# Local attention and MLP in one kernel: logits issued by pairs against logits issued after all products, subtraction in PSUM, and a new order of the work

## The chip, the cores and the metric

The kernel runs on one core of a Trainium2 chip. The metric is the device time of one execution in microseconds, lower is better. Engines are named as in the profile: PE does the matmuls (PEld its weight loads), DVE is the vector engine, ACT the scalar engine, POOL and SP mainly issue DMAs here.

## What is computed

x has 2048 rows of 640 bf16 numbers. With xn = layernorm(x), the output is x + A(xn) + B(xn).

```python
# A: 32 heads of 20 numbers; each row looks at 8 rows, 0, 2, ... 14 rows back
q, k, v = split(xn @ wqkv)                       # [32, 2048, 20] each
logits = einsum("bhsd,bhswd->bhsw", q, k[rows s - 2*w]) * 20 ** -0.5
logits = where(s - 2*w >= 0, logits, -1e9)
attn = softmax(logits over w)                    # w = 0..7
A = einsum("bhsw,bhswd->bhsd", attn, v[rows s - 2*w]) @ wo
# B: an MLP with 1536 hidden numbers
B = gelu_tanh(xn @ w1 + b1) @ w2 + b2
```

## The kernel before, in words

The 2048 rows are cut into four chunks of 512 (n = 0 to 3), each of four blocks of 128 rows (bl). Everything is held transposed: 128 partitions carry a slice of the 640 features (in five slices, t), the free axis carries the chunk's rows. The work is cut into 569 pieces, each a closure that issues a few instructions. A hand-held list, `ORDER`, gives the order in which all pieces are issued; every engine executes its own pieces in just that order, waiting by semaphore for what the pieces read and for the buffers they write. (`make_plan` also holds a cost and a rank for each piece, but when `ORDER` is given only the pieces' functions are used. POOL is not in the list of engines whose order is fixed by hand.) A piece's name is its kind, the chunk, and an index:

- `st`, `rs`, `rc`, `xn`, `tc`: row statistics (DVE, L403), square root (ACT, L424), reciprocal (DVE, L428), normalised rows (ACT, L440), and the transposing DMA into `xnT` (SP, L471). In chunk 0 matmuls transpose instead (`tp`), and its projections are cut smaller (`ga` to `ge`, `hj`, with their copies `gc`, `hc`).
- `pj n which to`: five matmuls of 128x512 for one slice of q, k or v (which = 0, 1, 2; PE, L503), and `pc`: its copy out of PSUM to bf16 (ACT, L562). `pad`: the 14 rows carried over from the chunk before.
- `qk n wp i`: q times k shifted by 2*(2*wp+i) rows, 2560 numbers per partition (DVE, L577), into a `prod` tile; one tile holds the pair i = 0, 1, so a chunk has four. The pool has four such tiles.
- `lg n wp`: the sums over each head: matmuls with a 128x32 matrix of zeros and ones (PE, L599), 256 columns each, in four column strips, 20 of them for each wp, into the PSUM tile `L` (one buffer, 8 offsets x 128 columns). In the kernel before, `lg03` does all 80 of chunk 0; in the other chunks `lg n1` does the 40 of wp 0 and 1, and `lg n3` those of wp 2 and 3.
- softmax: `mk` the mask of chunk 0 (L594), `m` the maximum (L612), `mx` the subtraction (L619), all DVE; `ex` the exponential (ACT, L629); `ss`, `ri`, `at` sum, reciprocal and product (DVE, L635 to L647).
- `xd`, `xs`: the attention weights are spread over partitions by four DMAs into `ax` (one buffer): two issued by SP (`xd`), two by ACT (`xs`, L657).
- `av n wp i`: v shifted, times `ax` (DVE, L673), into `prod` tiles; `ad` adds tiles pairwise (DVE, L682; three for a chunk), `ot` makes the result `oT` (DVE, L688).
- `f1 n ft`: five matmuls of 128x512 for one of twelve hidden slices (PE, L695), `ge`: gelu (ACT, L706), into `hT`.
- `o n bl pc`: for one block of 128 output rows, pc = 0 to 3 are three pairs of matmuls each (512 and 128 columns, L726 and L728) with `hT` and w2; pc = 4 is five such pairs with `oT` and wo, so it needs `ot n`. `oc`: copies out of PSUM (ACT, L733 and L734). `od`: POOL's DMA that adds them to the output in HBM (L739).
- `xp n`: an SP DMA that writes the chunk's rows of x to the output (L480); `xb n`: a POOL DMA that adds b2 to them (L484). `od` comes after `xb` of its chunk.

`pj`, `f1` and the small tiles of chunk 0 share four PSUM buffers ("acc"), so PE can be at most four such pieces ahead of ACT. `osb`, which `oc` fills and `od` empties, has two buffers; the PSUM tiles of `o` have one pair.

Of the kernel before, what the change touches and what calls it, by code (L numbers as in the profile page):

```python
# [62 lines left out]
S, D, F, H, W, DIL = 2048, 640, 1536, 32, 8, 2  # L63
P = 128
# [12 lines left out]
LASTB = S // P - 1  # L77
# [8 lines left out]
tc01a tc01b gb4 gd gc0 ge st02a hj100 gc4 st02 st03a hj102 st03 hc100 hj101 rs02 rs03 rc02 hc102 rc03 hj200 xn03 gc1  # L86
xn02 hc101 st10a tp02 tp03 st13a tc02 hj201 st10 tc03 st11a hj202 hc200 st11 hj112 hc202 st12a hj012 st13 hc112
hj010 st21a hj011 hc010 st12 hc012 st20a hj111 hc201 st32a rs1 st23a rc1 hj211 st21 hc111 hc011 st23 hj110 xn11 st20
st22a f105 hc110 st22 tc11 pad11 qk001 hj210 xn10 rs2 f102 hc211 b1 qk021 hc210 f100 ge05 tc10 rc2 qk000 f101 ge00
f104 qk031 xn12 f108 ge02 tc12 qk010 f107 ge08 ge01 st30a f109 qk011 xn13 f103 ge07 tc13 qk020 f106 ge03 qk030 f1010  # L90
ge06 ld ge04 pj110 st31a xn22 lg03 ge010 pc110 ge09 pj113 mk m0 pj102 pc113 mx0 pj112 pc102 st30 ex0 pj104 st32
st33a pj114 st33 st31 pc112 tc22 pj100 pc104 ss0 rs3 pj103 ri0 pj101 pc114 at0 pc100 pj111 pc103 pc101 rc3 xd0 f1011
pc111 xs0 qk100 pj123 ge011 pj122 qk111 f114 xn21 qk121 hj212 ge14 xw0 o000 hc212 qk110 xn20 pj121 tc20 qk101 o001
pc121 pj124 av030 pj120 pc124 pc122 qk120 tc21 lg11 xn23 av031 f112 f117 av020 ge12 tc23 pc120 f115 pc123 av000 f110
av001 f111 ge10 ge15 o002 av021 pad21 ge11 f113 pad12 xn33 ad01 o003 tc33 pj213 pj201 pc213 av011 pj210 pc201 xp0
av010 pj200 pc210 ge13 pj203 ad00 pc200 xn32 pj211 pj212 pc211 tc32 qk130 pj202 pc212 pj204 qk131 pc202 pc203 pj224
xb0 ad02 pj221 pc224 pc204 lg13 pc221 pad22 ot0 pj223 pj214 m1 o004 pc214 mx1 pc223 pj222 qk201 oc00 ex1 o010 od00
qk200 o011 o012 ss1 o013 o014 ri1 f1111 at1 oc01 xn31 o020 qk210 xd1 pc222 o021 pad31 xn30 o022 qk211 xs1 o023 qk231
o024 qk230 lg21 oc02 xw1 od02 o030 qk220 od01 f124 ge111 tc31 qk221 f119 ge17 av131 f1110 ge24 tc30 lg23 av110 f126
m2 o031 mx2 xp1 o032 ge26 ge19 pj220 av111 ex2 o033 av130 pj312 pc220 av120 pj310 xp2 pj311 pc310 ss2 f116 pc311 ri2  # L100
ge110 pj301 av121 o034 pc312 at2 pj302 oc03 av100 pc301 od03 pj313 pc302 pj303 av101 f118 pc303 ad11 xd2 pc313 pj314
ge18 xs2 f125 ge16 ad10 pj300 ge25 pj323 pc300 xw2 o100 pc323 ad12 pj322 xp3 o101 f127 av211 o102 pj320 av230 o103
xb1 pc320 ot1 pc314 f122 ge27 f1210 av201 ge22 o104 av231 pj304 oc10 av210 pad32 o110 o111 av221 o112 av220 o113 xb2
o114 av200 f1211 oc11 ad20 pc322 od11 o120 pc304 f123 o121 ad21 f120 o122 ge20 o123 qk301 o124 xb3 qk300 f132 oc12
od12 o130 qk310 o131 ge210 od10 ge32 qk311 o132 o133 ad22 f121 lg31 ge21 ge23 o134 qk321 f133 qk320 oc13 f128 ge33
qk331 ge211 pj321 qk330 f129 pc321 ge28 f130 ot2 ge29 lg33 ge30 o200 m3 pj324 mx3 o201 pc324 f135 ex3 o202 o203 ss3
o204 ri3 f131 oc20 at3 od20 f134 ge31 od13 xd3 o210 o211 xs3 o212 o213 o214 xw3 f1311 oc21 od21 o220 f1310 av300
o221 ge310 av311 o222 o223 av310 o224 av321 f139 oc22 av320 ge35 o230 f136 av330 o231 ge36 av331 ge311 f138 ge39
f137 ge34 ad31 o232 ge37 ge38 o233 o234 av301 o310 oc23 ad30 o330 od23 o311 od22 o331 o300 ad32 o301 o302 o312 ot3
o313 o303 xl o304 o314 oc30 od30 o320 oc31 o321 od31 o322 o323 o324 o332 oc32 o333 od32 o334 ohi oclo ochi  # L110
""".split()


def make_plan(fns, offsets={}):

    pl = Plan(offsets)
# [6 lines left out]
    def f(kind, *a):  # L123
        return lambda: fns[kind](*a)
# [15 lines left out]
    for n in range(NCH):  # L140
        base = n * PERIOD
# [65 lines left out]
        for which, buf in enumerate((q, k, v)):  # L207
# [5 lines left out]
            if which:  # L213
                need = done(n - 1, which) if n else []
# [21 lines left out]
        pl.add(f"mx{n}", VE, 1.22, n - 1000, [f"m{n}"], f("sub", n), [L, m, z])  # L236
        pl.add(f"ex{n}", SE, 1.02, n - 1000, [f"mx{n}"], f("exp", n), [z, e], table="exp")
# [22 lines left out]
        for bl in range(BPC):  # L260
# [22 lines left out]
def kernel(  # L283
# [16 lines left out]
    nc = tc.nc  # L300
# [91 lines left out]
    tiles = {}  # L392

    def get(key, make):
        if key not in tiles:
            tiles[key] = make()
        return tiles[key]
# [73 lines left out]
        nc.sync.dma_start_transpose(xnT[:, :, bl * P : (bl + 1) * P], tiles["xn", n, bl][:])  # L471


    def rows(n):
        cs = slice(n * BPC, min((n + 1) * BPC, LASTB))
        return cs, out_sd.rearrange("(b p) d -> p b d", p=P)[:, cs, :]

    def do_xp(n):
        cs, dst = rows(n)
        nc.sync.dma_start(dst, x_sb[:, cs, :])  # L480

    def do_xb(n):
        cs, dst = rows(n)
# [112 lines left out]
    def logits(L, prod, wp):  # L596
        for t in range(KT):
            for j in range(BPC):
                nc.tensor.matmul(  # L599
                    L[j * H : (j + 1) * H, 2 * wp : 2 * wp + 2, :],  # L600
                    lhsT=head_of[:],
                    rhs=prod[:, :, t, j * P : (j + 1) * P],
                    start=(t == 0 and wp % 2 == 0),
                    stop=(t == KT - 1 and wp % 2 == 1),
                    skip_group_check=True,
                )
# [7 lines left out]
        )  # L614

    def do_sub(n):
        z = prodp.tile([P, W, P], F32, tag="prod", name="z")
        tiles["z", n] = z
        nc.vector.tensor_tensor(  # L619
            out=z[:],  # L620
            in0=tiles["L", n][:],
            in1=tiles["m", n][:].unsqueeze(1).to_broadcast([P, W, P]),
            op=ALU.subtract,
        )

    def do_exp(n):
        e = smp.tile([P, W, P], BF16, tag="e", name="e")
        tiles["e", n] = e
        nc.scalar.activation(e[:], tiles["z", n][:], ACT.Exp, scale=SCALE)  # L629
# [173 lines left out]
```

## Time and profile before

| what | us |
|---|---|
| median of 13 runs | 215.03 |
| lowest and highest of them | 213.76, 218.82 |
| the profiled execution | 214.75 |
| its span in the profile | 212.6 |
| busy: PE, DVE, ACT, POOL | 206.6, 173.9, 108.8, 19.7 |
| granted TensorE clock | full in all slices |
| first and last matmul of the program proper (start; end) | 5.5; 209.4 |

The span runs from the first instruction to the last; the time of the execution is 2.15 us longer. A line of a list of groups gives line, engine, operation, tile written and tiles read, count, then busy time and the mean of one in ns. In the lists in order of time the first number is the start and the second the length, both in us. "A <- B: 0.3, 1, 0.3" among the waits means that A's engine sat idle 0.3 us in total, once, until B was done. A matmul's printed length (379 ns for 512 columns) includes the time to drain; starts that follow each other without a gap are 216 ns apart for 512 columns.

### The profile page before, as it was taken

How to read it: one execution, taken by the hardware profiler on the slowest of the kernel's cores; microseconds unless marked ns; L12 is line 12 of the kernel's file. 1: busy time of each engine (PE TensorE's matmuls, PEld its weight loads, DVE VectorE, ACT ScalarE, POOL GpSimd, SP SyncE). 2: the span in 40 equal slices, each digit the busy share in tenths (PEclk: the TensorE clock that was granted, in tenths of full speed). 3: DMA queues.
4: the chain of work that ended last, by engine and by line, in shares of the span. 5: the costliest groups of instructions: out<-in, count | busy, mean ns of one | idle time of the engine just before them, and what ended most of it. 6: DMA issues, size and time to landing. Idle time of an engine off the chain costs nothing.

```text
span 212.6 us, 3639 instructions
## 1 busy us (share of the span) xinstructions
PE 206.6 (97%) x1511; PEld 118.1 (56%) x1534; DVE 173.9 (82%) x178; ACT 108.8 (51%) x191; POOL 19.7 (9%) x37
## 2 busy tenths in 40 slices
PE   8999999999999999999999999999999999999993
PEld 2999645655555555555545455545545555455552
DVE  3586997798999999897999999999996606999401
ACT  5586988596746654557277514134264621550210
POOL 2000000000000200111221002111010101101111
PEclk9999999999999999999999999999999999999999
DMA  6999416957321490269996666220220083202053
GB/s 217 366 362 371 81 31 167 387 67 183 76 34 31 127 151 3 31 89 185 296 155 98 124 193 92 34 31 0 34 32 3 0 195 66 34 0 31 0 65 62
DMA packets 24120, 23.93 MB, mean 113 GB/s; under 512 B 9128, under 2 KB 21928, under 8 KB 24104
## 3 DMA queue, kind: packets, MB, share of 16 engines
q1 hardware_dynamic: 18520, 16.49, 28.5%
q0 software_dynamic: 4144, 4.92, 18.4%
q10 hardware_dynamic: 1440, 2.29, 3.3%
q8 instruction: 12, 0.20, 0.4%
q14 instruction: 4, 0.03, 0.0%
HBM read 10.00 MB, written 7.54 MB: 82 GB/s over the span
## 4 chain that ended last, share of the span: by engine, by line
PE 71%; DVE 14%; DMA 8%; ACT 3%; issue 2%; ACTq 0%; DVEq 0%
PE pps L503 21%; PE hps L695 18%; PE lo L726 15%; DMA ax<-attn 7%; PE gps L547 6%; DVE pv L673 6%; PE hi L728 4%; DVE pv L682 4%; PE L L599 3%; PE gps L516 1%; DMA x_sb<-in_A_x_dram 1%; ACT e L629 1%; PE tp L459 1%; DVE oT L688 1%; ACT L629 1%
## 5 line engine op out<-in xcount | busy, mean ns | idle before, releaser
L695 PE MATMUL hps<-xnT,w_sb 128*128 128x512 bf16 x231 | 55.6, 379 | 0.4
L726 PE MATMUL lo<-w_sb,hT 128*128 128x512 bf16 x188 | 54.1, 379 | 0.1
L673 DVE TENSOR_TENSOR pv<-vT,ax 128x2560 bf16<-128x2560 bf16 x32 | 45.7, 1482 | 8.8 <-DMA ax<-attn 7.2
L577 DVE TENSOR_TENSOR prod<-qT,kT 128x2560 bf16<-128x2560 bf16 x32 | 45.7, 1483 | 1.0 <-ACT kT L562 0.9
L706 ACT ACTIVATE hT<-hps,b1T 128x512 bf16<-128x512 f32 x48 | 31.4, 689 | 22.8 <-PE hps L695 16.3
L728 PE MATMUL hi<-w_sb,hT 128*128 128x128 bf16 x192 | 40.3, 219 | 0.3 <-issue 0.2
L695 PEld LDWEIGHTS <-w_sb 128*128 128x128 bf16 x240 | 22.6, 98 | 25.7 <-issue 0.4
L682 DVE TENSOR_TENSOR pv<-pv 128x5120 bf16<-128x5120 bf16 x12 | 33.7, 2822 | 0.2
L726 PEld LDWEIGHTS <-hT 128*128 128x128 bf16 x192 | 18.7, 98 | 22.2 <-issue 0.4
L733 ACT CAST osb<-lo 128x512 bf16<-128x512 f32 x15 | 8.8, 587 | 40.1 <-issue 18.5
L726 PE MATMUL lo<-wo,oT 128*128 128x512 bf16 x76 | 22.5, 379 | 0.2
L739 POOL DMA_DIRECT2D out_dram<-osb x15 | 13.0, 866 | 99.0 <-ACT osb L734 93.7
L728 PEld LDWEIGHTS <-hT 128*128 128x128 bf16 x192 | 18.4, 98 | 3.3
L503 PE MATMUL pps<-xnT,wk_sb 128*128 128x512 bf16 x74 | 18.3, 379 | 0.4 <-ACT vT L562 0.3
L503 PE MATMUL pps<-xnT,wv_sb 128*128 128x512 bf16 x72 | 18.0, 379 | 0.2
L503 PE MATMUL pps<-xnT,wq_sb 128*128 128x512 bf16 x73 | 17.7, 379 | 0.1
L403 DVE BATCH_NORM_STATS2 stats<-x_sb 128x6 f32<-128x320 bf16 x30 | 13.0, 467 | 5.7 <-DMA x_sb<-in_A_x_dram 5.7
L728 PE MATMUL hi<-wo,oT 128*128 128x128 bf16 x80 | 16.9, 219 | 0.3 <-issue 0.2
L562 ACT CAST vT<-pps 128x512 bf16<-128x512 f32 x15 | 8.6, 590 | 11.5 <-PE pps L503 11.5
L484 POOL DMA_DIRECT2D out_dram<-b2bc x4 | 5.3, 1324 | 88.7 <-DMA out_dram<-x_sb 88.7
L562 ACT CAST kT<-pps 128x512 bf16<-128x512 f32 x15 | 8.8, 585 | 9.2 <-PE pps L503 9.1
L726 PEld LDWEIGHTS <-oT 128*128 128x128 bf16 x80 | 7.8, 98 | 9.8 <-DVE oT L688 0.5
(73 smaller groups left out, 196.3 us busy)
## 6 DMA issues: line engine op xcount, KB each, us to landing
out_dram<-osb POOLq DMA_DIRECT2D x15, 160.0 KB, 3.5
ax<-attn SPq DMA_DIRECT2D x8, 256.0 KB, 5.3
ax<-attn ACTq DMA_DIRECT2D x8, 256.0 KB, 6.2
w_sb<-in_B_w_dram SPq DMA_DIRECT2D x2, 960.0 KB, 14.2
w_sb<-in_B_w_dram SPq DMA_DIRECT2D x1, 1920.0 KB, 8.7
out_dram<-x_sb SPq DMA_DIRECT2D x3, 640.0 KB, 5.2
out_dram<-b2bc POOLq DMA_DIRECT2D x3, 640.0 KB, 7.2
x_sb<-in_A_x_dram SPq DMA_DIRECT2D x1, 1280.0 KB, 13.4
```

Source lines behind the costliest of these rows:

```text
L403: nc.vector.bn_stats(stats[:, i, :], x_sb[:, b, i * (D // 2) : (i + 1) * (D // 2)])
L503: nc.tensor.matmul(ps[:], lhsT=wqkv_p[which][:, ti, to, :], rhs=xnT[:, ti, :], start=(ti == 0), stop=(ti == KT - 1),)
L547: nc.tensor.matmul(ps[:, to - a, :], lhsT=wqkv_p[which][:, ti, to, :], rhs=tiles["xnT", 0][:, ti, pair * 2 * P : (pair + 1) * 2 * P], star ...
L562: nc.scalar.copy(dest[:, to, off : off + CH], tiles["pps", n, which, to][:])
L577: nc.vector.tensor_tensor(out=prod[:, i, :, :], in0=qkv_tile(n, 0)[:], in1=qkv_tile(n, 1)[:, :, off : off + CH], op=ALU.mult,)
L673: nc.vector.tensor_tensor(out=pv[:, i, :, :].rearrange("p t (j c) -> p t j c", j=BPC), in0=qkv_tile(n, 2)[:, :, off : off + CH].rearrange( ...
L682: nc.vector.tensor_tensor(out=ta[:], in0=ta[:], in1=tb[:], op=ALU.add)
L695: nc.tensor.matmul(ps[:], lhsT=w1_sb[:, ti, ft * P : (ft + 1) * P], rhs=tiles["xnT", n][:, ti, :], start=(ti == 0), stop=(ti == KT - 1),)
L706: nc.scalar.activation(hT[:], tiles["hps", n, ft][:], ACT.Gelu_apprx_tanh, bias=b1T[:, ft : ft + 1], scale=1.0)
L726: nc.tensor.matmul(lo[:], lhsT=lhs, rhs=rhs[:, 0:CH], start=first, stop=last)
L728: nc.tensor.matmul(hi[:, 0 : D - CH], lhsT=lhs, rhs=rhs[:, CH:D], start=first, stop=last)
L739: nc.gpsimd.dma_start(rows, tiles["osb", n, bl][:], accum_op=ALU.add)
```

## The change

Three edits, and a new `ORDER` that goes with them.

1. The logits of every chunk are sixteen pieces (`lg n0` to `lg n3`), 20 matmuls each, and the planner lets the first of them start when all eight products of the chunk exist.
2. `mx` writes its result back to `L` in PSUM instead of to an SBUF tile `z` of the `prod` pool, and `ex` reads `L`.
3. `xp1` writes the rows of chunks 1 and 2 in one DMA; there is no `xp2`, and `xb2` depends on `xp1`.

```diff
-        pl.add(f"xp{n}", DQ, 4.3, base + 30, ["ld"], f("xp", n))
-        pl.add(f"xb{n}", DQ, 8.2, base + 33, [f"xp{n}"], f("xb", n))
+        first = 1 if n == 2 else n
+        if n == first:
+            pl.add(f"xp{n}", DQ, 8.2 if n == 1 else 4.3, base + 30, ["ld"], f("xp", n))
+        pl.add(f"xb{n}", DQ, 8.2, base + 33, [f"xp{first}"], f("xb", n))
...
-            group = 2 if n else 4
-            if wp % group == group - 1:
-                wps = range(wp - group + 1, wp + 1)
-                need = [f"qk{n}{x}{i}" for x in wps for i in range(2)] + ([f"lg{n}{wp-group}"] if wp > group else [])
-                every = [("prod", "qk", n, x) for x in wps]
-                pl.add(f"lg{n}{wp}", PE, 0.21 + 0.546 * group, n - 1000, need, f("lg", n, wps), every + [L], slack=0.8)
+        need = [f"qk{n}{x}{i}" for x in range(W // 2) for i in range(2)]
+        for wp in range(W // 2):
+            us, slack = (0.546, 0.0) if wp else (0.755, 0.3)
+            need = [pl.add(f"lg{n}{wp}", PE, us, n - 1000, need, f("lg", n, wp), [("prod", "qk", n, wp), L], slack=slack)]
...
-    def rows(n):
-        cs = slice(n * BPC, min((n + 1) * BPC, LASTB))
+    def rows(n, end):
+        cs = slice(n * BPC, min(end * BPC, LASTB))
...
     def do_xp(n):
-        cs, dst = rows(n)
+        cs, dst = rows(n, 3 if n == 1 else n + 1)
...
     def do_sub(n):
-        z = prodp.tile([P, W, P], F32, tag="prod", name="z")
-        tiles["z", n] = z
+        L = tiles["L", n]
         nc.vector.tensor_tensor(
-            out=z[:],
-            in0=tiles["L", n][:],
+            out=L[:],
+            in0=L[:],
...
-        nc.scalar.activation(e[:], tiles["z", n][:], ACT.Exp, scale=SCALE)
+        nc.scalar.activation(e[:], tiles["L", n][:], ACT.Exp, scale=SCALE)
```

The new `ORDER` moves most pieces. These are PE's pieces around the logits, before and after:

```
before  f1010 pj110 lg03 pj113                       pj120 lg11 f112 ... pj221 lg13 pj223
        o024 lg21 o030 ... f1110 lg23 f126           f121 lg31 o134 ... f130 lg33 o200
after   f101 lg00 lg01 lg02 pj113 lg03 pj102         pj124 lg10 pj122 lg11 lg12 o021 lg13 o022
        pj311 lg20 lg21 o010 lg22 o011 o012 pj302 lg23 o013
        o114 lg30 lg31 o120 lg32 lg33 o121
```

And stretches of the other engines after the change that the prediction speaks of:

```
DVE  st21a st12 st21 st32a st30a st32 st22a rc1 st23a qk011 qk001 b1 st23 qk030 qk010 qk031 qk021 qk020 qk000
     ... at0 [eight qk1] av011 av010 av021 av001 av030 m1 av000 av031 mx1 av020 ad01 ad00 ad02 ot0 ss1 ri1
     qk221 qk231 qk211 at1 qk200 qk220 qk210 qk230 qk201 av101 av120 av131 av121 m2 av110 mx2 av100 av111
     av130 ad10 ss2 ri2 ad11 at2 qk320 ad12 qk331 qk321 ot1 qk311 qk330 qk301 qk300 qk310 av200 av230 av201
     m3 mx3 av231 av221 av211 av210 av220 ss3 ri3 at3 ad21 ad20 ad22 ot2 xl [chunk 3: eight av, three ad, ot3]
ACT  ... pc300 pc312 pc304 xs1 pad31 oc00 ...    oc12 pc324 ex3 ge25 ...
SP   ... tc33 xp0 xd1 xp1 xp3 xd2 xd3
POOL xb0 od02 xb1 xb2 od00 xb3 od01 ...          (as built)
```

Before, chunk 3's products came after chunk 2's `av` and `ad20 ad21`, and DVE's end read `ot2 m3 mx3 ss3 ri3 at3` and then chunk 3's eight `av`.

More of the change, by code (lines that the diff above doesn't have):

```diff
@@ L85 @@
 pad01 pad02 st00a st00 sm rs00 me nm rc00 sq xn00a xn00b tp00a tp00b tc00a rs01 ga tc00b rc01 xn01 gb2 tp01 gb3
[L86 to L109, printed above, removed]
@@ L110 @@
-o313 o303 xl o304 o314 oc30 od30 o320 oc31 o321 od31 o322 o323 o324 o332 oc32 o333 od32 o334 ohi oclo ochi
+tc01a tc01b gb4 gd gc0 ge st03a hj101 gc4 st03 st02a rs03 hj100 hc101 rc03 xn03 gc1 st02 hj102 hc100 hj202 rs02 tp03
+rc02 hj201 xn02 tc03 st11a st12a hc102 tp02 hc202 st10a hj200 tc02 st11 st13a hj112 hc200 st13 hj110 hc112 st10
+hc201 hj111 st21a st12 hj010 hc111 st21 rs1 st32a hj011 hc010 st30a st32 hc110 hj012 st22a hc011 hj210 rc1 hc012
+st23a xn10 qk011 hj211 hc210 tc10 xn12 f100 qk001 hc211 f108 b1 st23 ge00 f102 qk030 tc12 f1010 ge08 qk010 xn11 f104
@@ new lines @@
+ge02 qk031 tc11 f107 ge04 ge010 qk021 f105 xn13 hj212 ge07 tc13 qk020 f1011 hc212 f109 qk000 f101 ge09 ld st20a
+ge011 st33a lg00 st22 pad12 ge01 lg01 st31a pad11 st30 lg02 ge05 pj113 st20 st33 rs2 lg03 st31 pj102 mk pc113 rc2
+pj103 m0 pc102 rs3 pj111 mx0 pc103 xn20 pj114 pc111 ex0 pj100 tc20 pj112 pj101 pc100 ss0 pc112 pj110 xn22 rc3 pc114
+ri0 tc22 pj104 pc101 at0 pc110 f113 pc104 qk120 f106 ge13 xd0 f103 qk100 ge06 pj121 qk110 xs0 f111 ge03 qk131 pj120
+ge11 xn21 xw0 f115 qk101 pc121 pc120 f112 qk111 pj123 ge12 qk130 xn23 o020 pc123 tc23 f118 qk121 pj124 lg10 xn31
@@ new lines @@
+tc21 pj122 av011 lg11 pc122 av010 lg12 ge15 o021 pc124 av021 tc31 xn32 lg13 o022 av001 o023 f110 av030 tc32 pj214 m1
+pj213 pc214 ge10 av000 pj202 ge18 xn30 pj211 av031 pc213 tc30 pj203 pc202 pc211 mx1 xn33 pj210 av020 pj204 pc210
+tc33 pc203 ad01 pj220 pad21 f114 pc220 pc204 pj201 ex1 xp0 ad00 pj221 pj200 pc201 pc221 pj212 ad02 pj222 xb0 pc212
+pc200 pj224 pad22 ot0 pj310 pc224 pc222 pj223 ss1 pj301 pc223 ri1 o024 pc301 qk221 pc310 pj304 oc02 qk231 o000 od02
+o001 qk211 pj303 at1 o002 pc303 pj300 qk200 xd1 o003 pc300 qk220 pj312 qk210 f1111 pc312 pc304 pj314 xs1 qk230 o004
@@ new lines @@
+pad31 xw1 qk201 pj311 oc00 xp1 pc314 lg20 lg21 av101 o010 lg22 av120 o011 o012 av131 pj302 av121 lg23 pc302 o013
+pc311 m2 o014 av110 xb1 pj313 oc01 mx2 od01 o030 f117 ge14 od00 av100 o031 av111 ge17 o032 f119 av130 f1110 ge19
+ad10 pc313 o033 ex2 pj323 xp3 f120 pc323 ss2 o034 ge20 ri2 pj320 oc03 ad11 f130 ge110 od03 f116 ge30 ge111 f121
+pc320 at2 f1210 ge21 qk320 xd2 pj321 ge210 xs2 ad12 pj324 pc321 f123 ge16 f128 ge23 qk331 xw2 o100 qk321 f125 xb2
+o101 ot1 o102 o103 qk311 o104 qk330 pj322 oc10 qk301 ge28 od10 o110 pc322 o111 qk300 o112 o113 qk310 xb3 o114 lg30
@@ new lines @@
+oc11 lg31 av200 od11 o120 lg32 av230 lg33 o121 av201 o122 o123 m3 o124 mx3 f126 oc12 av231 pc324 od12 o130 ex3 av221
+o131 o132 av211 f1310 ge25 f129 av210 ge26 f1211 av220 pad32 ge29 f122 ss3 o133 ge22 ge211 f124 ri3 f127 at3 f139
+ge27 ad21 xd3 f135 o134 ge35 ge24 ad20 f137 oc13 xs3 o210 ge310 f1311 xw3 ad22 o211 o212 f138 ot2 o213 ge38 ge37 xl
+o214 av301 f131 oc21 av321 ge311 od21 o220 av311 o221 od13 o222 av330 o223 o224 av300 f132 oc22 av310 od22 o230 ad30
+o231 o232 o233 o234 av320 f136 oc23 av331 o200 ad31 o201 ge31 ge39 f133 ge32 f134 ge33 ad32 ge36 o202 ge34 o203 o310
@@ L111 @@
+o311 o204 o330 ot3 oc20 o331 od20 o300 od23 o301 o302 o303 o304 o312 oc30 o313 od30 o320 o321 o314 o322 oc31 o323
+od31 o324 o332 oc32 o333 od32 o334 ohi oclo ochi
 """.split()
@@ L223, in make_plan @@
                 pl.add(f"qk{n}{wp}{i}", VE, 1.42, base + 3.0 * wp + i, need, f("qk", n, wp, i), [q, k, pr])
-            group = 2 if n else 4
-            if wp % group == group - 1:
-                wps = range(wp - group + 1, wp + 1)
-                need = [f"qk{n}{x}{i}" for x in wps for i in range(2)] + ([f"lg{n}{wp-group}"] if wp > group else [])
-                every = [("prod", "qk", n, x) for x in wps]
-                pl.add(f"lg{n}{wp}", PE, 0.21 + 0.546 * group, n - 1000, need, f("lg", n, wps), every + [L], slack=0.8)
+        need = [f"qk{n}{x}{i}" for x in range(W // 2) for i in range(2)]
+        for wp in range(W // 2):
+            us, slack = (0.546, 0.0) if wp else (0.755, 0.3)
+            need = [pl.add(f"lg{n}{wp}", PE, us, n - 1000, need, f("lg", n, wp), [("prod", "qk", n, wp), L], slack=slack)]
         e, at, ax = ("e", n), ("attn", n), ("ax", n)
-        m, rs, ss, z = ("m", n), ("rs", n), ("ss", n), ("prod", "z", n)
+        m, rs, ss = ("m", n), ("rs", n), ("ss", n)
         if n == 0:
@@ L235, in make_plan @@
         pl.add(f"m{n}", VE, 1.22, n - 1000, [f"lg{n}3"] + ([] if n else ["mk"]), f("max", n), [L, m])
-        pl.add(f"mx{n}", VE, 1.22, n - 1000, [f"m{n}"], f("sub", n), [L, m, z])
-        pl.add(f"ex{n}", SE, 1.02, n - 1000, [f"mx{n}"], f("exp", n), [z, e], table="exp")
+        pl.add(f"mx{n}", VE, 1.22, n - 1000, [f"m{n}"], f("sub", n), [L, m])
+        pl.add(f"ex{n}", SE, 1.02, n - 1000, [f"mx{n}"], f("exp", n), [L, e], table="exp")
         pl.add(f"ss{n}", VE, 1.51, n - 1000, [f"ex{n}"], f("sum", n), [e, ss])
@@ L471, in do_td @@
         nc.sync.dma_start_transpose(xnT[:, :, bl * P : (bl + 1) * P], tiles["xn", n, bl][:])
-    def rows(n):
-        cs = slice(n * BPC, min((n + 1) * BPC, LASTB))
+    def rows(n, end):
+        cs = slice(n * BPC, min(end * BPC, LASTB))
         return cs, out_sd.rearrange("(b p) d -> p b d", p=P)[:, cs, :]
     def do_xp(n):
-        cs, dst = rows(n)
+        cs, dst = rows(n, 3 if n == 1 else n + 1)
         nc.sync.dma_start(dst, x_sb[:, cs, :])
     def do_xb(n):
-        cs, dst = rows(n)
+        cs, dst = rows(n, n + 1)
         nc.gpsimd.dma_start(dst, b2bc[:].unsqueeze(1).to_broadcast([P, cs.stop - cs.start, D]), accum_op=ALU.add)
@@ L585, in do_b1, with do_lg @@
         nc.vector.tensor_copy(b1T[:], b1_t[:, 0:FT])
-    def do_lg(n, wps):
+    def do_lg(n, wp):
         L = get(("L", n), lambda: psL.tile([P, W, P], F32, tag="L", name="L"))
-        for wp in wps:
-            logits(L, tiles["qk", n, wp], wp)
+        logits(L, tiles["qk", n, wp], wp)
     def do_mask():
```

## Prediction, on record before the changed kernel ran

> **What bounds the kernel now.** First the page's busy times, then the chain that ended last by engine: PE is busy 97% of the span and holds 71% of the chain.
>
> ```profile
> PE 206.6 (97%) x1511; PEld 118.1 (56%) x1534; DVE 173.9 (82%) x178; ACT 108.8 (51%) x191; POOL 19.7 (9%) x37
> ...
> PE 71%; DVE 14%; DMA 8%; ACT 3%; issue 2%; ACTq 0%; DVEq 0%
> ```
>
> A busy matmul can hide stalls, so next the list of PE's waits (total, times, longest), the start-up among them:
>
> ```profile
> PE idle L768 <- PEq L787: 0.8, 1, 0.8
> PE hi L728 <- issue: 0.3, 2, 0.2
> PE tp L459 <- DVE xn L444: 0.3, 1, 0.3
> PE pps L503 <- ACT vT L562: 0.3, 1, 0.3
> ```
>
> Then the chain in order of time, for the pitch of matmuls, which no drain blurs:
>
> ```profile
> 35.16 1.08 PE pps L503 x5
> 36.24 2.30 PE L L599 x80
> 38.54 0.34 PE pps L503
> ...
> 79.51 1.21 PE L L599 x40
> ```
>
> Five matmuls of 512 columns take 1.08, so 0.216 each; a 512+128 pair takes 0.27 (three: 0.82, five: 1.36). In PE's timeline the last ordinary matmul before logits starts at 95.53, the first after 40 of them at 96.89:
>
> ```profile
> 95.53 0.22 PE L728 MATMUL hi<-wo,oT 128*128 128x128 bf16 x1
> 95.68 1.28 PE L599 MATMUL L<-prod,head_of 128*32 128x256 bf16 x40
> 96.89 0.39 PE L726 MATMUL lo<-w_sb,hT 128*128 128x512 bf16 x1
> ```
>
> That run occupies 96.89-95.53-0.06 = 1.30. The 80 of chunk 0 occupy 2.39 (start of the last pj110 matmul 35.86 plus 0.216, to 38.47). Both fit 0.0273 per matmul plus **0.21 per unbroken run**. PE's list from 5.5 on: 465 matmuls of pj and f1 100.4, 272 pairs of o 74.0, logits 8.7+7x0.21 = 10.2, chunk 0's transposes and smaller projections 17.9: it would end at 208.0; PE really ends at 209.3, drain left off. So before loses just 1.25 to all waits: about 0.25 at the start, 0.25 at 109, 0.2 late, the rest crumbs. That is all a new order can win.
>
> DVE is second: between 110 and 160 it has almost no gap. Its prices come from the groups (busy, mean ns) less 0.07 overlap when back to back:
>
> ```profile
> L673 DVE TENSOR_TENSOR pv<-vT,ax 128x2560 bf16<-128x2560 bf16 x32 | 45.7, 1482 | 8.8 <-DMA ax<-attn 7.2
> L577 DVE TENSOR_TENSOR prod<-qT,kT 128x2560 bf16<-128x2560 bf16 x32 | 45.7, 1483 | 1.0 <-ACT kT L562 0.9
> L682 DVE TENSOR_TENSOR pv<-pv 128x5120 bf16<-128x5120 bf16 x12 | 33.7, 2822 | 0.2
> ```
>
> av and qk 1.41, ad 2.81, ot 1.48; from the same list m 1.22, sub 1.25, the three sums 1.4, reciprocal 0.98, attn 1.22.
>
> **What the Trainium skill says.** Trainium Kernel Development and Optimization, Performance Expectations, calls matmul busy time a bad metric for closeness to roofline because matmuls are pipelined; the trace agrees (379 ns printed, 216 ns pitch), hence my sums by pitch. TensorE: Matmul & The Clock Gate, Back-to-back issue gap, gives N/2.4+2.5 ns: 216 and 56 ns for 512 and 128, as measured here; it prices no switch into column strips, so the 0.21 is this trace's own. ScalarE: Activation LUTs, What ACT_TABLE_LOAD costs, puts a switch of tables at about 2.66 us with a drain; here a load takes 1.28 and the activation follows at once, so I use 1.28. DMA: Bandwidth & Descriptors, Issuing engines are not separate DMA queues, says DMAs of all issuers share 16 engines and interleave; the trace's 3.9 to 9.2 us for equal ax DMAs agrees.
>
> **The change, part by part.** *Logits.* Despite the change's words, the built program has ten unbroken runs, not four: other matmuls stand between (pj113; pj122 and o021; o010 and o011 to pj302; o120). Before had seven. 3 x 0.21 = **+0.63** on PE, with nothing beside it to hide it, as PE is the chain. Both ends: 0 if the price belongs to a chunk, 0.8 if each run costs 0.03 more, as the matmul after it sometimes does. I take 0.63. PE's own list then sums to 208.6.
>
> *Chunk 0.* lg00 waits for qk000, now DVE's last product. DVE is held for x until 18.39 in both. From there eight half statistics at 0.42, three aggregates at 0.2 and rc1 at 0.3 reach 22.65 for qk011; eight products at 1.41, b1 0.08 and st23 0.62 reach 34.6, so PE can start logits at 34.7. PE's list puts f101's end at 34.1, plus the 0.25 already lost at the start, 34.4. **+0.3**. (f104 meets about the same 0.3 earlier, since ACT's gelu table waits for b1 after two products; and f108, which needs w1's second half, moves from 28.5 to 24.2, where that load, issued at 10.13, lands at about 24.3 by its row's 14.2. Both lie inside the 0.3, as PE meets them before lg00.) Range 0 to 0.7, as rows of the start-up shift by some tenths.
>
> *Products all before logits.* The four prod tiles are then full, so DVE's next av stands until the first lg has run; each chunk starts a race between DVE and PE at lg n0. DVE's first av starts 0.97 after it (0.21+0.55+0.16 drain+0.05).
> From lg10 to lg20, DVE: 8 av, 8 qk, 3 ad, ot, m, sub, softmax 3.6 = 38.5, with 0.97: 39.5. PE: 27 pieces of 1.08, seven o of 0.82, two of 1.36, logits 2.8 = 40.4. Cover 0.9; cost 0.
> From lg20 (time t) to o104, which needs ot1. DVE: 8 av 11.3, 3 ad 8.4, 3 qk 4.2, ot 1.5, m and sub 2.5, softmax 3.6 = 31.5, so t+32.45. PE: 17 x 1.08, 12 x 0.82, 2 x 1.36, logits 2.8 = t+33.65. Cover 1.2, if ax1 lands by t+2.2.
> It may not: xs1, half of ax1, sits in ACT's queue behind pc312, whose pj312 is done at t-4.4, although at1 is done at t-8. ACT's sequencer waits there, as at 48.42, where xs0 went out only when pc111's matmuls were done:
>
> ```profile
> 48.42 0.59 ACT L562 CAST kT<-pps 128x512 bf16<-128x512 f32 x1
> 48.42 2.13 ACTq L657 DMA_DIRECT2D ax<-attn  x2
> ```
>
> Second issue at t-3.7, landing after the page's median:
>
> ```profile
> ax<-attn ACTq DMA_DIRECT2D x8, 256.0 KB, 6.2
> ...
> out_dram<-x_sb SPq DMA_DIRECT2D x3, 640.0 KB, 5.2
> ```
>
> t+2.5: **+0.3**. Range 0 (3.9 us) to 3.3 (9.2 us).
> From lg30 to o214, which needs ot2. DVE: 8 av, 3 ad, ot, m, sub, softmax = 27.3, plus 0.97: 28.2. PE: 12 x 1.08, 12 x 0.82, 2 x 1.36, 2.6 = 28.1. **+0.15**.
>
> *ACT.* As many table loads, 11. Behind oc12: pc324, load, ex3, load, ge25 end 13.05 after lg30, where f1211 wants ge25's buffer at 12.95; behind oc03, ge20 and ge110 free theirs for f130 and f116 within 0.1 of when PE wants them, though before o104 that hides in its wait. Together **+0.2**, 0 to 0.6. PE's `o` pieces stand in line behind a late f1, as all of PE does.
>
> *Chunk 3's softmax.* DVE's 7.2 wait for ax3 goes, since ad2 and ot2 now fill it; ot3 comes 4.7 before o304. But PE waited only some 0.08 there: worth 0.1. Next late is o214, above.
>
> *Subtraction in PSUM, exp from it.* The mask (L594) already works in place on L: 287 ns for 128 numbers against 1224 for the subtraction's 1024 is 1.05 ns per number, the same rate; ACT's copies from PSUM (590 ns at 512, 273 at 128) extend to 1.01 at 1024, against exp's 1.06. Zero, within 0.1 each way for each of four. L is held to exp, with over 10 us before the next lg. If a PSUM-to-PSUM subtraction took 0.1 more, DVE's covers shrink by 0.1 and o214 pays it. A gain beside it: ex2 waited for two things, so its table load stood behind the wait; now exp has one wait and the load runs ahead. Before:
>
> ```profile
> 106.57 1.28 ACT L629 ACT_TABLE_LOAD   x1 [1.48 <-DVE z L619]
> ...
> 109.44 1.24 PE L503 MATMUL pps<-xnT,wk_sb 128*128 128x512 bf16 x5 [0.25 <-ACT vT L562]
> ```
>
> PE's 0.25 there goes: **-0.25**. ACT next waits for av130 (pc323 takes its v buffer), 1 us before PE wants it. Another 0.1 of late crumbs go with their old places.
>
> *One DMA for two chunks.* Saves an issue of about 0.5 on SP, which has slack: 0. POOL's xb1, then xb2, od00, xb3, od01 queue behind the longer transfer. Issued at t-6.5, it lands near t+1; two b2 additions took until 9.3 after the second's issue before, so od00 is down near t+14; oc03 needs that buffer at t+20. Cover 6, cost 0. It also shares the DMA engines with ax1's late half: that is the 9.2 end above.
>
> Sum: 0.63+0.3+0.3+0.15+0.2-0.25-0.1-0.1 = **+1.15**: the profiled execution's 214.75 (span 212.6 plus 2.15) becomes 215.9. The median of the runs is 0.28 higher, so 216.2.
>
> **Rivals.** *Not slower (215.3).* The buffers hold: ax1 lands before t+2.2, DVE's products end before 34.4, ACT hands over in time. Left are 0.63 less 0.35. For it: each of these waits is under 0.4 and rests on sums good to 0.3. Against: four such races must all be won. It decides at ax1 plus 2.2. If the 0.21 is paid per chunk (the split costs nothing), 215.0.
> *ax1 late (219.2).* The half behind pc312 takes 9.2 us, as the slowest before; o104 then waits 3.3 in place of 0.3. For: xp1 and xp3, 1.7 MB, go out just before it. Against: the transposing DMAs that shared chunk 1's time before are now earlier.
> *A gain (213.8).* The median before lies 1.27 above its lowest run, 213.76. If that spread is ax3's landing, which stood right on the path, the cover of 4.7 removes it: 213.76+0.28 = 214.0, or 213.4 were the runs free; I count 213.8. Against: PE's list leaves no more, and ax1 is exposed instead.
>
> **How the numbers follow.** Forecast 0.52 (own range 215.5 to 217.2), not slower 0.22, ax1 late 0.20, gain 0.06. A measurement tells about 0.5%, 1.08 us, from no change, so the forecast lies just past that line: 0.32 of its 0.52 is slower, 0.20 same. Faster 0.06, same 0.42, slower 0.52. From 214.9 to 218.8: below lie the gain and some of the second case, above half of the late one.
>
> **What would show it.** Ten runs of L599, each 0.21 above its matmuls; PE idle before lg00 on DVE prod; DVE idle on ax1 past t+2.2 and PE idle at o104 on DVE oT; no PE wait near ex2; DVE's 7 us gap gone with no gain. I am wrong if PE's list stays dense (not slower), or if PE waits on ACT or POOL where I gave cover.

## The result, and the profile after

| | kernel before | changed kernel |
|---|---|---|
| median | 214.84 (48 runs) | 217.13 (11 runs) |
| lowest | 213.76 | 216.57 |
| ratio after/before, with its 95% interval | | 1.0127 [1.0097, 1.0156] |
| profiled execution; its span | 214.75; 212.6 | 218.01; 215.9 |

The change costs about 2.3 us, near 1.1%. The side and the range (214.9 to 218.8) held; the size did not: the prediction's sum was +1.15, half of what came. The ratio is taken over fast executions alone, so it is not the quotient of the two medians. The profiled execution of the changed kernel is 0.9 above its own median; its late start alone is worth that much (below).

The page of the changed kernel, busy times and the chain by engine, to be laid beside the prediction's first fence:

```profile
PE 207.1 (96%) x1510; PEld 117.4 (54%) x1534; DVE 173.4 (80%) x178; ACT 108.6 (50%) x191; POOL 19.8 (9%) x37
...
PE 78%; DVE 11%; DMA 7%; ACTq 1%; issue 1%; ACT 0%; SPq 0%; DVEq 0%
```

PE is as busy as it was, in a span that is 3.3 longer: it got little more work (0.63 by the prediction's count), it waited more. So the list of waits comes next (total, times, longest):

```profile
DVE pv L672 <- DMA ax<-attn: 6.4, 1, 6.4
...
PE gps L517 <- DMA wq_sb<-in_A_wqkv_dram: 1.7, 1, 1.7
...
PE hps L694 <- ACT vT L563: 1.4, 1, 1.4
...
ACT vT L563 <- DVE pv L672: 0.8, 1, 0.8
...
PE hps L694 <- ACT hT L705: 0.5, 1, 0.5
```

The 1.7 is the load of wq at the start: the instructions there are the same in both kernels, so it is this execution's draw. PE's other two new waits are on ACT, and ACT's is on DVE, which had stood 6.4 for `ax`. Read from the bottom up that is one chain. To place it, I laid PE's starts against its own list without gaps (each piece at the prices of the prediction, from 5.5 on). PE runs 1.9 behind from the start-up on and stays there until 122; then it loses 0.8 at `f130` and `f116`, 1.57 at `f128`, 0.13 at `f1211` (158.8), and nothing more. So nearly all that the change costs beyond its longer list falls between 122 and 134.

The source is chunk 1's weights. SP's issues, its half of `ax` (L656) and then xp1 and xp3 (L481):

```profile
94.35 1.22 SPq L656 DMA_DIRECT2D ax<-attn  x2
95.62 3.23 SPq L481 DMA_DIRECT2D out_dram<-x_sb  x2
```

ACT's timeline, with its half (`xs1`) behind pc312 (98.22):

```profile
98.22 0.59 ACT L563 CAST kT<-pps 128x512 bf16<-128x512 f32 x1 [1.31 <-PE pps L504]
98.38 0.55 ACTq L656 DMA_DIRECT2D ax<-attn  x1
...
98.97 1.50 ACTq L656 DMA_DIRECT2D ax<-attn  x1
```

And DVE's first `av` of chunk 1:

```profile
107.68 1.49 DVE L672 TENSOR_TENSOR pv<-vT,ax 128x2560 bf16<-128x2560 bf16 x1 [6.35 <-DMA ax<-attn]
```

`lg20` starts at t = 102.71, so the second issue is at t-3.74, just where the prediction had it (t-3.7). But the half is down at t+5.0 and not at t+2.5: 8.7 after that issue, not 6.2. The trace's packets show the crowd: ACT's half moves from 102.56 to 107.24, and xp1 and xp3 (issued from 95.62, 1.7 MB) from 98.34 to 107.03. POOL issues the addition of b2 to the rows of chunk 1 at 104.60, but its first packet moves at 106.50, too late to count for much here. Of the 8.9 from the first issue to the last packet, 4.2 pass before the first packet moves.

What then holds PE up is ACT's queue. ACT's and PE's timelines around 133 (two views):

```profile
130.20 2.38 ACTq L656 DMA_DIRECT2D ax<-attn  x2
132.62 0.59 ACT L563 CAST vT<-pps 128x512 bf16<-128x512 f32 x1 [3.28 <-PE hps L694]
```

```profile
133.25 1.24 PE L694 MATMUL hps<-xnT,w_sb 128*128 128x512 bf16 x5 [1.41 <-ACT vT L563]
```

DVE is 4 late, so `at2` is done only at 130.16; `xs2` waits for it in ACT's queue and then takes 2.38 to issue; `pc321` stands behind it until 132.62; `f128` needs the buffer that `pc321` frees. (The bracket of the second line names PE, which had long been done; the ACTq line above it is what stood in the way.)

### The profile page after: what moved, and what is told of

Its sections match the earlier page's. It is cut to its first block, busy times and chain, and to the rows that moved or that the text cites. A ratio compares the mean times of both kernels' runs of the same rounds, so it can differ in the third digit from the quotient of the medians.

```text
span 215.9 us, 3639 instructions
## 1 busy us (share of the span) xinstructions
PE 207.1 (96%) x1510; PEld 117.4 (54%) x1534; DVE 173.4 (80%) x178; ACT 108.6 (50%) x191; POOL 19.8 (9%) x37
## 4 chain that ended last, share of the span: by engine, by line
PE 78%; DVE 11%; DMA 7%; ACTq 1%; issue 1%; ACT 0%; SPq 0%; DVEq 0%
PE lo L725 23%; PE hps L694 19%; PE pps L504 19%; PE hi L727 7%; PE gps L548 6%; DVE pv L672 5%; DMA ax<-attn 4%; PE L L599 3%; DMA wq_sb<-in_A_wqkv_dram 3%; DVE pv L681 3%; PE gps L517 1%; ACTq L656 1%; DVE L L618 1%; DVE attn L646 1%; DVE m L612 1%
## 5 line engine op out<-in xcount | busy, mean ns | idle before, releaser
L725 PE MATMUL lo<-w_sb,hT 128*128 128x512 bf16 x183 | 52.9, 379 | 0.0
L738 POOL DMA_DIRECT2D out_dram<-osb x15 | 14.1, 940 | 98.4 <-ACT osb L733 98.4
L725 PE MATMUL lo<-wo,oT 128*128 128x512 bf16 x79 | 23.0, 379 | 0.0
L504 PE MATMUL pps<-xnT,wq_sb 128*128 128x512 bf16 x74 | 18.5, 379 | 0.1
L563 ACT CAST qT<-pps 128x512 bf16<-128x512 f32 x15 | 8.9, 592 | 11.9 <-PE pps L504 11.8
L485 POOL DMA_DIRECT2D out_dram<-b2bc x4 | 5.8, 1585 | 93.0 <-DMA out_dram<-x_sb 93.0
```

What stands on the lines that cost most here:

```text
L504: nc.tensor.matmul(ps[:], lhsT=wqkv_p[which][:, ti, to, :], rhs=xnT[:, ti, :], start=(ti == 0), stop=(ti == KT - 1),)
L563: nc.scalar.copy(dest[:, to, off : off + CH], tiles["pps", n, which, to][:])
L725: nc.tensor.matmul(lo[:], lhsT=lhs, rhs=rhs[:, 0:CH], start=first, stop=last)
L738: nc.gpsimd.dma_start(rows, tiles["osb", n, bl][:], accum_op=ALU.add)
```

## The experiments

All are timed against the kernel before on the same chip, whose medians in these sessions were 214.7 to 215.1. Unless said, each is the changed kernel with one edit of `ORDER`.

| kernel | median | ratio to before |
|---|---|---|
| e1 xs1 early | 214.29 | 0.9978 [0.9956, 1.0] |
| e2 xp1, xp3 early | 214.08 | 0.9974 [0.9948, 1.0] |
| e3 four runs of logits | 216.57 | 1.0079 [1.0053, 1.0105] |
| e4 xs2 late | 216.86 | 1.0114 [1.0068, 1.0159] |
| e5 xs1 early, four runs | 213.14 | 0.9923 [0.9896, 0.9951] |
| e6 xs1 early, fourteen runs | 215.28 | 1.003 [1.0007, 1.0054] |
| e7 xp split | 220.56 | 1.0251 [1.0206, 1.0297] |
| e9 before, subtraction in PSUM | 214.97 | 1.0003 [0.9974, 1.0031] |
| e10 xs issued by SP | 214.02 | 0.9989 [0.9962, 1.0016] |
| e11 xs1 early, xp split | 214.67 | 1.0009 [0.9981, 1.0037] |

**e1, the place in ACT's queue.**

```diff
-pc303 pj300 ... pc300 qk220 pj312 qk210 f1111 pc312 pc304 pj314 xs1
+pc303 xs1 pj300 ... pc300 qk220 pj312 qk210 f1111 pc312 pc304 pj314
```

> The changed kernel with one step moved: ACT's two issues for chunk 1's weights (xs1) stand right behind pc303, ahead of pc300, pc312 and pc304, so that they go out when at1 is done (94.3) and not at 98.4. Theory (ax1 is late because of its place in ACT's queue, and DVE's 6.35 wait for it is handed on as PE's 2.35): second issue near 96, ax1 down by 102 to 103, DVE's wait on ax1 under 1.5, PE's waits at f130, f116 and f128 gone, 2.0 to 2.4 less than the changed kernel's 217.1, so 214.7 to 215.1. Rival (the traffic of xp1 and xp3 is what makes it late): ax1 still down only at 105 to 107, less than 0.8 gained, 216.3 or more. Rival (the loss is in the ten runs of logits and in chunk 0): no gain, 217.

Measured: 214.29, 2.84 less than the changed kernel. ACT's timeline, then DVE's:

```profile
92.69 0.59 ACT L563 CAST qT<-pps 128x512 bf16<-128x512 f32 x1 [3.09 <-PE pps L504]
92.85 2.19 ACTq L656 DMA_DIRECT2D ax<-attn  x2
```

```profile
101.75 5.70 DVE L672 TENSOR_TENSOR pv<-vT,ax 128x2560 bf16<-128x2560 bf16 x4 [2.16 <-PE L L599]
```

DVE no longer waits for `ax` but for the first `lg` of chunk 2, as the prediction's race has it, and PE's lag behind its list is 0.33 at the end, 0.16 of it from the start. The half's packets end at 99.93, 7.1 after the first issue, with the same xp1 and xp3 beside them: slow still, but early enough. Here 2.5 pass before the first packet moves, and 4.6 while they move.

**e2, the traffic.**

```diff
-... xp0 ad00 ... xp1 pc314 ... xp3 f120
+... xp0 xp1 xp3 ad00 ... pc314 ... f120
```

> The changed kernel with xp1 and xp3 (SP) put right behind xp0, so that they go out near 77.7 and are down before at1 is; xs1 stays behind pc312. Theory (place in the queue and traffic both count): issues of ACT's half still at 98.4 and 100.5, but its landing then takes about 4 and not 8.7 after the first issue, ax1 down near 104 in place of 107.2, DVE's wait near 3.2, and PE gets 1.0 to 1.8 back: 215.3 to 216.1. Rival (place alone): landing and time unchanged, 216.8 to 217.3. Rival (traffic alone): DVE's wait falls under 1.5 and all 2.3 comes back, 214.8.

Measured: 214.08, all of the loss back, more than my theory allowed (1.0 to 1.8). `xs1` still goes out behind pc312, at 96.90 and 97.49, but its packets end at 101.99, 5.1 after the first issue and not 8.9. DVE:

```profile
102.44 4.30 DVE L672 TENSOR_TENSOR pv<-vT,ax 128x2560 bf16<-128x2560 bf16 x3 [2.59 <-DMA ax<-attn]
```

`lg20` starts at 101.23 here, so DVE could not have begun before 102.2 (t+0.97) in any case: the 2.59 that the profile puts down to `ax` costs 0.2. This is what the rival "traffic alone" forecast, and yet e1 with the same xp1 and xp3 shows that the place alone is a cure too. The half is late only when it is issued late and into a crowd, and either cure is enough. The DMA engines were not empty in e2: POOL's additions of b2, moved ahead together with xp1 and xp3, ran on to 100.40. The half's first packet moves 2.7 after its issue, at 99.58, and the rest takes 2.4, against 4.2 and 4.7 in the changed kernel.

**e3, the logits truly together.**

```diff
-f101 lg00 lg01 lg02 pj113 lg03         lg10 pj122 lg11 lg12 o021 lg13
-lg20 lg21 o010 lg22 o011 o012 pj302 lg23       lg30 lg31 o120 lg32 lg33
+f101 lg00 lg01 lg02 lg03 pj113         lg10 lg11 lg12 lg13 pj122 o021
+lg20 lg21 lg22 lg23 o010 o011 o012 pj302       lg30 lg31 lg32 lg33 o120
```

> The changed kernel with the 80 logits matmuls of each chunk truly together: pj113, pj122 and o021, o010, o011, o012 and pj302, and o120 go out behind the last lg of their chunk; four runs and not ten. Theory (each run costs PE 0.21 that nothing hides): PE's list shorter by 6 x 0.21 = 1.26; ax1 stays as late as it is against PE's clock, or later by 0.2, so 1.0 to 1.3 less, 215.8 to 216.1, and PE's waits at f130, f116, f128 stay or grow by up to 0.3. Rival (the price belongs to a chunk or the late ax1 hides it all, since PE then waits that much longer on DVE): 216.8 to 217.1.

Measured: 216.57, 0.56 less: less than I expected. PE's list is 1.26 shorter, but DVE waits 7.2 for `ax` (6.4 in the changed kernel), and PE has a new wait on ACT beside those at `f128` and `f130`:

```profile
DVE pv L672 <- DMA ax<-attn: 7.2, 1, 7.2
...
PE pps L504 <- ACT vT L563: 1.3, 1, 1.3
```

What PE saves ahead of a wait that DVE sets is handed back in that wait. What the runs are worth had to be measured without it:

**e5 and e6, the price of a run.** Both are e1 with the logits regrouped: e5 has e3's four runs; e6 cuts chunks 1 to 3 as far as they go.

```diff
-lg10 pj122 lg11 lg12 o021 lg13 o022    lg20 lg21 o010 lg22 o011 o012 pj302 lg23    lg30 lg31 o120 lg32 lg33 o121 o122
+lg10 pj122 lg11 o021 lg12 o022 lg13    lg20 o010 lg21 o011 lg22 o012 pj302 lg23    lg30 o120 lg31 o121 lg32 o122 lg33
```

> xs1 right behind pc303, and the 80 logits matmuls of each chunk together: four runs in place of ten. With xs1 early PE had only 0.33 of waits left in all (214.3). Theory (0.21 for each run, nothing beside it): 6 x 0.21 = 1.26 less, 213.0, with PE's waits still under 0.6; four runs alone had given only 0.56 because the rest went into a longer wait for ax1. Rival (the price of a switch is small and 0.56 was all of it): 213.7. Rival (PE ahead by 1.26 meets DVE at o104 or o214, whose cover was under 0.3): PE waits 0.5 or more there, 213.5 to 214.

> xs1 right behind pc303, and the logits of chunks 1 to 3 cut as far as they go: a piece of o between every two lg (o021, o022; o010, o011, o012; o120, o121, o122), fourteen runs and not ten. Theory (0.21 for each run): 4 x 0.21 = 0.84 more than the 214.3 of ten runs, 215.1; from four to fourteen runs 2.1 in all. A part of it may be a wait for DVE, since the last lg ends some 2 later: up to 0.3 more. Rival (no price for a run): 214.3.

Measured: 213.14 with four runs, 214.29 with ten, 215.28 with fourteen: 1.15 for six runs (0.19 each), 0.99 for four (0.25 each). e5 and e6 were timed in one session and differ by 2.14 for ten runs, so 0.214 each. The chain of e5 at the logits of chunk 2, and below it that of the changed kernel around those of chunk 1:

```profile
100.67 2.30 PE L L599 x80
```

```profile
62.36 0.66 PE L L599 x20
...
64.22 1.21 PE L L599 x40
...
66.35 0.66 PE L L599 x20
```

80 matmuls take 2.30 in one run and 0.66+1.21+0.66 = 2.53 in three, and that leaves out the part of the price that falls on the matmul ahead of each run. e5 is also the best kernel here, 0.8% under the kernel before.

**e4, where a late DVE is met.**

```diff
-pj321 ge210 xs2 ad12 pj324 pc321 f123 ge16 f128
+pj321 ge210 ad12 pj324 pc321 f123 ge16 xs2 f128
```

> The changed kernel with ACT's two issues for chunk 2's weights (xs2) behind pc321 and ge16, so that pc321 no longer stands behind an issue that waits for at2 (130.2). Theory (PE's 1.57 at f128 is only the first place where a late DVE is met; o104, which needs ot1, waits for the same lateness a few pieces on): PE's wait at f128 falls under 0.3, and a wait for oT of about 1.4 appears at o104; no gain over 0.3, 216.8 to 217.2. Rival (the loss is ACT's queue order at that place, and DVE had cover for o104): 1.3 to 1.6 gained, 215.5 to 215.8.

Measured: 216.86, 0.27 less. PE's wait at `f128` is gone, and `o104` has one in its place:

```profile
138.22 0.39 PE L725 MATMUL lo<-wo,oT 128*128 128x512 bf16 x1 [1.30 <-DVE oT L687]
```

So ACT's queue only took from PE, a few pieces early, what `o104` would have taken.

**e7 and e11, the merged transfer.** The third edit undone: e7 in the changed kernel, e11 in e1.

```diff
+        pl.add(f"xp{n}", DQ, 4.3, base + 30, ["ld"], f("xp", n))
+        pl.add(f"xb{n}", DQ, 8.2, base + 33, [f"xp{n}"], f("xb", n))
...
+        cs, dst = rows(n, n + 1)
...
-oc00 xp1 pc314
+oc00 xp1 xp2 pc314
```

> The changed kernel with its third edit undone: xp1 and xp2 are two DMAs again, one right behind the other at xp1's place on SP. Theory (it is where the new order puts this traffic, right behind xd1, that counts, and not how it is cut): ax1 as late as before within 1, DVE's wait 5 to 7.5, 216.6 to 217.4. Rival (the long merged DMA holds the DMA engines): DVE's wait under 3, 215 to 215.8.

Measured: 220.56, 3.4 worse than the changed kernel by the medians, a miss for both theories. POOL's timeline, first of e7 and then of the changed kernel (L483 and L485 are the additions of b2):

```profile
101.20 1.30 POOL L483 DMA_DIRECT2D out_dram<-b2bc  x1 [9.67 <-DMA out_dram<-x_sb]
104.26 1.28 POOL L483 DMA_DIRECT2D out_dram<-b2bc  x1 [1.76 <-DMA out_dram<-x_sb]
```

```profile
104.60 2.61 POOL L485 DMA_DIRECT2D out_dram<-b2bc  x2 [12.06 <-DMA out_dram<-x_sb]
```

Two transfers land one after the other, so POOL's first addition starts 3.4 earlier (2.4 by the start of `lg20`), and its packets move from 104.00 on, not from 106.50. They join the crowd around ACT's half: its packets go from 99.77 to 107.78, 10.4 after the first issue, and DVE waits 8.09. In this profile PE's waits after `f101` are 1.7 longer than in the changed kernel's, and the end of the program is 0.4 longer (see e11). That makes 2.1. The median says 3.4 because four of e7's six executions were granted a TensorE clock of only 0.984 or 0.992, against one of twelve of the changed kernel. The other two took 219.19 and 219.50, which is 2.1 and 2.4 above the changed kernel's median. Whether the edit brings the lower clock was not tested.

> xs1 right behind pc303, and the third edit undone (xp1 and xp2 two DMAs, one behind the other). Undone with xs1 late it cost 3.4, since xb1 then started at 101.2 and not at 104.6 and its traffic met ACT's half of ax1 too. Theory (it matters only for a half of ax1 that is still on its way then): with xs1 early nothing is left of that, 214.0 to 214.6. Rival (split transfers, or xb's place on POOL, cost by themselves): 215.5 or more, and a PE wait that is not on ax1's path.

Measured: 214.67, against 214.29 with the merged DMA. The intervals of the two ratios overlap, and PE loses no more after `f101` than in e1: as a guard for a half that is late the merge is no longer needed. But the traces show that the 0.4 is real, and that it lies behind all matmuls. The last output DMA in e1 (span 211.84) and in e11 (span 214.99):

```profile
209.46 0.35 ACTq L758 DMA_DIRECT2D out_dram<-osb  x1
```

```profile
212.17 0.36 ACTq L756 DMA_DIRECT2D out_dram<-osb  x1
```

From this issue to the end are 2.38 in e1 and 2.82 in e11. It is so in every trace here: from the start of the last matmul to the end of the span are 3.39 to 3.41 in the four kernels with split transfers (before, e7, e9, e11) and 2.96 to 2.99 in the eight with the merged one. At its end SP checks the counters that tell of the DMAs' landing, one check after another, 0.06 apart and always in the same order. With the split transfers the last output DMA is counted where the second check looks: it lands 1.32 before the end of the span, and the seven checks behind it still follow. With one DMA fewer it is counted where the last check looks, and little follows its landing. So the merge is worth 0.43 here at the end of the program, by the place that the last DMA has in a list.

**e9, the subtraction alone.** The kernel before, in its own order, with the second edit.

```diff
-        z = prodp.tile([P, W, P], F32, tag="prod", name="z")
-        nc.vector.tensor_tensor(out=z[:], in0=tiles["L", n][:], ...
+        nc.vector.tensor_tensor(out=L[:], in0=L[:], ...
...
-        nc.scalar.activation(e[:], tiles["z", n][:], ACT.Exp, scale=SCALE)
+        nc.scalar.activation(e[:], tiles["L", n][:], ACT.Exp, scale=SCALE)
```

> The kernel before, in its own order, with the second edit alone: the maximum is subtracted in place in PSUM and exp reads PSUM. Theory (both rates are the same, 1.22 and 1.06; at ex2 the table load no longer stands behind the second wait, and PE's 0.25 there goes): 214.5 to 215.0, 0 to 0.4 less than before. Rival (PSUM is slower for DVE or ACT, or the buffer z that left the ring of prod tiles lets products start elsewhere): over 0.5 from before's median.

Measured: 214.97 beside 214.7, a ratio of 1.0003: no difference that can be told. The subtraction takes 1.23 (before 1.23), exp 1.02 (before 1.06), and PE's 0.25 at `ex2` is gone from the list of waits. But another stands there in this execution, 0.9 for chunk 1's `oT` at `o104`, and behind it DVE's for chunk 1's `ax`:

```profile
127.62 2.89 DVE L672 TENSOR_TENSOR pv<-vT,ax 128x2560 bf16<-128x2560 bf16 x2 [2.50 <-DMA ax<-attn]
```

In the kernel before's own trace these two start at 126.59 without a wait. So already in the old order one `ax` landed with next to no slack. The second edit was tried in the old order alone; undone in the new one it was not run.

**e10, the issuing engine.**

```diff
-        expand(nc.scalar, n, (2, 3))
+        expand(nc.sync, n, (2, 3))
```

> The changed kernel with the second half of every chunk's weights (xs) issued by SP, right behind the first half (xd), so that no part of ax stands in ACT's queue; xp1 and xp3 follow behind it on SP; ten runs of logits. Theory (place in ACT's queue is what made the half late; who issues it doesn't matter): four issues near 92.6 to 95, ax1 down before the first lg of chunk 2 has run, DVE's wait on ax1 under 1.5, 214.0 to 214.6, as with xs1 early on ACT. Rival (two queues are needed to bring 1 MB down in time, or issues on SP hold the transposes of chunk 2 up): ax1 down at 103 or later, or a new wait of PE on xnT; 215 or more.

Measured: 214.02. With all four issues on SP, behind each other, DVE begins chunk 1's `av` at 102.17, when the first `lg` has run (`lg20` at 101.38), and PE ends 0.72 behind its list, 0.58 of it from the start. One issuing engine brings `ax` down in time; it is not the second queue that counts, but what the half stood behind.

## Why the prediction was half right

| term | forecast | what the runs show |
|---|---|---|
| three more runs of logits | +0.63 | +0.64 (3 x 0.214; e1, e5, e6) |
| ax1's half behind pc312 | +0.3 | +2.84 (medians, changed kernel less e1); 2.3 in the two traces from `f101` on |
| chunk 0, `lg00` on `qk000` | +0.3 | nothing at `lg00`; 0.16 (e1) and 0.27 (e2) at `f104`, which the prediction put inside the same 0.3 |
| `o214` on `ot2` | +0.15 | 0 (lag 0.37 at `o214`, 0.39 at `f1211` before it, e1) |
| ACT's handovers | +0.2 | +0.13, all at `f1211` (changed kernel) |
| `ex2`'s table load | -0.25 | the wait is gone (changed kernel and e9) |
| late crumbs, chunk 3's softmax | -0.2 | more than that (below) |
| one DMA for two chunks | 0 | -0.43 at the end of the program (e11 less e1, traces) |

**The step that failed** is "Second issue at t-3.7, landing after the page's median: ... t+2.5: +0.3". The issue came at t-3.74; the landing took 8.7 and not 6.2. The same paragraph had the cover right: `ax` by t+2.2 costs nothing, and landing 2.8 past that cost 2.84 by e1's median, 2.3 by the two traces. The case called *ax1 late* describes what happened, 9.2 and 3.3 in place of 8.7 and 2.84, and it got a chance of 0.20. The reason to give it more was in the prediction's own text: xp1 and xp3, 1.7 MB, go out on SP just ahead. I set against it that the transposes were now earlier, and took the row's median, which is taken over eight issues with different neighbours. In e2, where xp1 and xp3 had gone ahead, the same late half needs 4.9 from its second issue to DVE's start, and t+1.2 lies inside the cover. Issued at this place, the half took either well under the median (4.9) or far more (8.7), by its neighbours. The sharing of the DMA engines, for which the prediction cites the skill, shows here with its size: 5.1 (e2), 7.1 (e1), 8.9 (changed kernel) and 10.4 (e7) from first issue to last packet for the same 512 KB, by what else was under way.

**The place was wrong too**, without changing the size. The prediction let `o104` wait on `oT`. In the changed kernel PE lost it earlier, through ACT's queue (`pc323` behind `av130`, `pc321` behind `xs2`); e4 took one of these away and the wait appeared at `o104`. The prediction had looked at ACT's waits with DVE on time, and had not asked what a late DVE does to the queue of an engine that waits for it in order.

**The small terms were too dear**, and that hid part of the miss. The eight terms add up to 1.13 (the prediction has 1.15), so without ax1's the sum was +0.83. e1, which has everything else of the change, stands at -0.55 (214.29 against 214.84), and its profiled execution 0.71 below the one before. Chunk 0, `o214` and ACT's handovers were charged 0.65 and came to about 0.3. And the kernel before lost, by the same lags, 0.33 up to `f101` and 1.31 by the end; e1 loses 0.16 and 0.33. So the new order wins 0.8 of 0.98 lost after the start, where the prediction credited 0.45. Last, the merged DMA's 0.43 at the end of the program was not in the sum at all. Together these account for e1's profile: 0.64 for the longer list, less 0.98 for all waits, less 0.43, is -0.77, against the -0.71 of the profiled executions. The case *not slower* had the races right, all but ax1's, within 0.3.

**The 0.21 per run** was right, and so was that the built kernel has ten of them. The Trainium skill's TensorEngine Tiling (Array Packing), Key Properties, says that changing the tiling mode drains TensorE; it gives no figure, and the runs put 0.214 on one run of 128x32 strips, there and back. Whether that drain is all of it no run here separates. As to the pitch, the formula that the prediction takes from the Trainium skill's TensorE: Matmul & The Clock Gate, Back-to-back issue gap, is given there for an isolated matmul; for a stream with weight loads the same section has about 131 ns at 512 columns and 81 at 128. The stream of this case shows 216 and 56, and the sums rest on these.

**Chunk 3's softmax** went as said: DVE's 7.2 wait is gone, and PE had next to nothing to gain there. **The merged DMA** was costed at 0. With the late half it spared 1.7 of waits by holding POOL's additions back (e7), and with the half late or early 0.43 at the end of the program (e7, e11); no step of the prediction saw either.

Open: why the half's first packet moved only 4.2 after its first issue in the changed kernel and 2.4 in e7, where transfers of x stand ahead of it in both; and whether place and traffic both mended give more than either (not run together, but e1 and e2 leave PE only 0.2 to 0.3 of waits after the start).

## What to carry to other kernels

When a change moves a DMA issue, price its landing with what is queued around it at that moment, on all issuers, and not with the median of its row; then ask how far past its cover the slow end lies. A DMA issue in a compute engine's queue had two costs here: it started as late as what it stood behind (`xs1` behind `pc312`), and what stood behind it started as late as what it waited for (`pc321` behind `xs2`). Before regrouping work to shorten the bounding engine's list, remove the waits that another engine sets, or the saving is handed back in them (0.56 of 1.26 in e3, 1.15 once the wait was gone).

## What the runs showed that I had not expected

*The start-up is a draw.* Up to `f101` PE has the same instructions in all kernels of the new order, but its lag there ran from 0.16 (e1) over 0.38 to 0.89 (seven others) to 1.9 (the changed kernel) and 2.8 (e11). In the changed kernel it is PE's first wait, for wq:

```profile
7.95 1.03 PE L517 MATMUL gps<-xnT,wq_sb 128*128 128x128 bf16 x15 [1.74 <-DMA wq_sb<-in_A_wqkv_dram]
```

In e11 that wait is shorter, 1.12, and the rest of the 2.8 is the clock. From 7.2 to 10.6 PE was granted half of it, which for 3.4 us is worth about 1.7 by estimate; the page shows it in the second of its 40 slices:

```profile
7.24 1.79 PE L515 MATMUL gps<-xnT,wq_sb 128*128 128x128 bf16 x15 [1.12 <-DMA wq_sb<-in_A_wqkv_dram]
```

```profile
PEclk9699999999999999999999999999999999999999
```

In e1 and e2, which started early, 0.16 and 0.27 of the lag is lost at `f104`: ACT's gelu table load waits for b1 on DVE, as the prediction said. ACT's timeline of e1:

```profile
25.26 1.28 ACT L705 ACT_TABLE_LOAD   x1 [0.63 <-DVE b1T L586]
```

All this is more than most edits here are worth, so two profiled executions are compared from `f101` on, and kernels by their medians.

*An issue is not free for the engine that makes it.* The second DMA of `xs1` held ACT for 1.50 in the changed kernel, the pair for 2.19 in e1 and that of `xs2` for 2.38, where the kernel before shows 0.58 and 0.88 for `xs1` (but 2.13 for the pair of `xs0`). It isn't peculiar to ACT: SP's pair takes 1.22 in the changed kernel and 2.19 in e2. What makes an issue long was not tested.
